# Column sums of V's weights by DMA and GpSimd, block 3 turned by DMA, and a new order of the first loads

## The chip, the core and the metric

The kernel runs on one core of one Trainium2 chip. A core has TensorE (matrix products, which accumulate in PSUM), VectorE, ScalarE and GpSimd (elementwise work) and SyncE, which only issues transfers (DMAs). ScalarE and GpSimd can issue transfers too. Each engine runs its own list of instructions in order and waits for the others through semaphores. The metric is device time of one execution in microseconds; lower is better. In the profile the engines are called PE, DVE, ACT, POOL and SP, and PEld is TensorE's loading of weights.

## The reference

From one input x (2048 rows of 512, bf16) two branches are computed on the normalized rows, and added to x:

```python
xn = _layernorm(x, axis=-1)
return x + _A_ref(xn, A_wqkv, A_wo) + _B_ref(xn, B_w_in, B_w_sp, B_b_sp, B_w_out)
```

Branch A is attention with 32 heads of 16 values, in which row s looks at the 8 rows s, s-2, ..., s-14: q, k and v are xn times wqkv, the logits are q·k/4, a softmax runs over the 8 rows (those before row 0 are masked), the weighted sum of v follows, and then the product with wo. Branch B takes z = gelu(xn w_in), split in z1 and z2 of 896 columns each; z2 is normalized along its row; g = w_sp z2 + b_sp mixes the 2048 rows; and (z1 * g) w_out is the branch's result.

## The kernel before

**Tiling.** The 2048 rows are 16 blocks of 128 (index b), and 4 groups j of four blocks. xn is needed turned (512 values on partitions, rows along the free side), as xnT. Everything lies in one on-chip array, `arena`, of which regions are used again for other things later; `fpool` holds small float32 values, and PSUM has 8 banks of 512 float32 values per partition.

**Stages on TensorE.** First 8 matmuls on constants (`warm`, L560). Then for each block V (L654, `v_block`) and z2 (L766, `z2_block`), for each group Q and K (L677, `qk_pair`), then z1 (L812), then g = w_sp z2 (L907, from 98 us on), then the output blocks (L963, L972). L713 (`logits`) sums, for two groups at a time, the products of q and k over the 16 values of a head.

**Layer norm.** `ln_block(b)` takes the statistics of a block on VectorE (L599 `bnst`, L601 `bnag`, L609 `vpe`), 1/sqrt on GpSimd (L611 `rstd`), and normalizes on VectorE (L623 `norm`). Blocks 0 to 3 (`NXT`) are then turned by TensorE against a unit matrix (L579, `xTr`) and copied to xnT by ScalarE (L587, `xTe`); blocks 4 to 15 are turned by a DMA that SyncE issues (L617, `xTd`).

**V of blocks 0 and 1.** These two don't wait for their norm. The raw rows are turned (L579, `xTx`), copied by ScalarE (L606, `xTc`) and multiplied with V's weights (`wv`). As (x - m) r W = r (x W - m s), with s the column sums of W, the sums are needed: `colsum` multiplies a matrix of ones with `wv` on TensorE (L638, `cs_0` and `cs_1`, 4 matmuls), which leaves s on every partition, and ScalarE copies -s (L642, `cse`). VectorE adds -s m in PSUM (L660, `fix`), and ScalarE multiplies by r on the way out (L663, `Ve`). GpSimd then issues the store of the block's V to DRAM (L668, `Vw`; scratch `vscr`), from where SyncE loads shifted rows back for the attention sum (L930).

**VectorE's long part.** For each j and each of 4 sets of heads, one product of 4096 values per partition (L698) and, from the second set on, one sum (L703); L713 of groups 0 and 1 needs all eight products and six sums. The second norm works in waves of four blocks (`z2_wave`): four tiny steps on VectorE (L785 to L792), 1/sqrt on GpSimd (L795, `zr`), four normalizations on VectorE (L798, `zn`).

**What sets the order.** `Plan.schedule` simulates all engines with estimated durations (`est`), a model of the transfers, and the landing times in `land` for the first loads; at each step it places the task that can start first, and among those within `tol` ns the one with the smallest `prio`. VectorE's next task may begin `overlap` ns before the estimated end of the last. The result is one fixed list for each engine. For the opening the order is written out by hand (L1003 to L1012); `after` and these lists add order without a wait. The waits that the engines really carry out follow from the data alone. A task that uses PSUM gets a bank when it is placed.

**First loads.** SyncE issues wv in two halves, x of block 2, the two halves of w_in's second part (`w_in2a`, `w_in2b`, for z2), x of blocks 3 to 7, Q's weights, K's weights and x of blocks 8 to 15; ScalarE issues x of blocks 0 and 1. After the turns of blocks 4 to 15 come the turned loads of w_sp (L880), with w_in's first part (L853) among them.

## Time and profile before

| | us |
|---|---|
| median of 3 runs (lowest, highest) | 237.30 (237.21, 237.56) |
| span of the profiled execution, from first to last instruction | 236.1 |
| around the span (the runs' times less the span) | 1.1 to 1.5 |
| PE busy | 231.7 (98%) |
| DVE busy | 207.4 (88%) |
| ACT busy | 96.5 (41%) |
| POOL busy | 32.7 (14%) |
| granted TensorE clock | 1.000 |

The profile is of one execution. It gives no total time of that execution, so its span stands beside the three runs. In the lines of a timeline below, the first number is the start in us from the beginning of the span, the second the time from the start of the first instruction of the line to the end of its last, then come engine, line of the program, operation, output<-input with its shape, and the count; in square brackets stands how long the engine was idle before it, and what ended that. In a line of waits stand who waited, for whom, the total in us, how often, and the longest. Matmuls overlap: one is shown with 0.38 us, while the next starts 0.215 us after it.

### The profile page before, as it was taken

The page shows a single profiled execution, that of the slowest core. Times are in us where ns is not written, and L with a number is a line of the kernel's source. Part 1 is how long each engine was busy: PE and PEld are TensorE (multiplying, and loading weights), DVE is VectorE, ACT ScalarE, POOL GpSimd, SP SyncE. Part 2 cuts the span into 40 slices and gives each one's busy share as a digit, 9 for nine tenths or more (in the row PEclk, how much of TensorE's full clock was granted, in tenths as well). Part 3 has the DMA queues.
Part 4 walks back from the last instruction along what each step waited for, and adds up shares of the span by engine and source line. Part 5 has one row for each costly group of instructions (what it writes and reads, how often), then busy time and mean ns, then how long its engine had stood idle before and what let it go on. Part 6 is the DMA issues. An engine that isn't in the chain of part 4 may idle for free.

```text
span 236.1 us, 2974 instructions
## 1 busy us (share of the span) xinstructions
PE 231.7 (98%) x1114; PEld 109.1 (46%) x1135; DVE 207.4 (88%) x269; ACT 96.5 (41%) x145; POOL 32.7 (14%) x56
## 2 busy tenths in 40 slices
PE   8999999999999999999999999999999999999996
PEld 3455555555444444444444444444444444444443
DVE  3799899999998899999699998986989997999432
ACT  3598889888967895510120531111111111000000
POOL 2259650311733100000000000000000000000000
PEclk9999999999999999999999999999999999999999
DMA  7998969991048325430999999998995959936432
GB/s 211 352 283 163 243 146 217 195 202 44 22 165 260 92 85 69 104 118 0 226 347 252 225 266 180 200 304 187 346 258 175 261 161 303 193 95 181 135 96 69
DMA packets 82013, 43.86 MB, mean 186 GB/s; under 512 B 54336, under 2 KB 81360, under 8 KB 82000
## 3 DMA queue, kind: packets, MB, share of 16 engines
q1 hardware_dynamic: 80768, 41.27, 71.5%
q0 software_dynamic: 800, 2.11, 2.8%
q10 hardware_dynamic: 432, 0.30, 0.6%
q8 instruction: 9, 0.15, 0.3%
q14 instruction: 4, 0.03, 0.1%
HBM read 26.35 MB, written 4.21 MB: 129 GB/s over the span
## 4 chain that ended last, share of the span: by engine, by line
PE 94%; DMA 3%; SPq 1%; ACT 1%; issue 1%; DVE 0%
PE ps L907 41%; PE ps L677 12%; PE ps L972 10%; PE ps L812 10%; PE ps L766 9%; PE ps L963 6%; PE ps L654 5%; DMA arena<-in_B_w_in_dram 3%; PE ps L713 1%; ACT arena L774 0%; SPq L518 0%; ACT arena L587 0%; PE ps L579 0%; SPq L514 0%; SPq L524 0%
## 5 line engine op out<-in xcount | busy, mean ns | idle before, releaser
L907 PE MATMUL ps<-arena 128*128 128x512 bf16 x439 | 96.6, 379 | 0.5
L907 PEld LDWEIGHTS ps<-arena 128*128 128x128 bf16 x448 | 43.7, 98 | 53.1 <-issue 0.4
L915 ACT ACTIVATE arena<-ps 128x1024 bf16<-128x1024 f32 (+1 forms) x16 | 14.7, 917 | 78.0 <-PE ps L907 78.0
L698 DVE TENSOR_TENSOR arena<-arena 128x4096 bf16<-128x4096 bf16 x16 | 36.5, 2282 | 0.1
L935 DVE TENSOR_TENSOR arena<-arena 128x4096 bf16<-128x4096 bf16 x16 | 36.4, 2283 | 0.0
L938 DVE TENSOR_TENSOR arena<-arena 128x2048 bf16<-128x2048 bf16 (+1 forms) x32 | 29.9, 948 | 0.0
L677 PE MATMUL ps<-arena 128*128 128x512 bf16 x126 | 28.7, 379 | 0.1
L703 DVE TENSOR_TENSOR arena<-arena 128x4096 bf16<-128x4096 bf16 x12 | 27.4, 2287 | 0.1
L972 PE MATMUL ps<-arena 128*128 128x512 bf16 (+2 forms) x117 | 26.9, 366 | 0.1
L766 PE MATMUL ps<-arena 128*128 128x448 bf16 x128 | 26.0, 352 | 0.5 <-DMA arena<-in_B_w_in_dram 0.5
L812 PE MATMUL ps<-arena 128*128 128x512 bf16 x110 | 24.4, 379 | 0.1
L978 DVE TENSOR_TENSOR arena<-ps,arena 128x512 bf16<-128x512 f32 (+2 forms) x17 | 11.2, 658 | 11.7 <-PE ps L972 11.7
L677 PEld LDWEIGHTS ps<-arena 128*128 128x128 bf16 x128 | 14.5, 113 | 13.0
L766 PEld LDWEIGHTS ps<-arena 128*128 128x128 bf16 x128 | 12.3, 98 | 12.7 <-ACT arena L642 0.7
L686 ACT ACTIVATE arena<-ps 128x1024 bf16<-128x1024 f32 x16 | 16.3, 1021 | 4.4 <-PE ps L677 4.1
L972 PEld LDWEIGHTS ps<-arena 128*128 128x128 bf16 x119 | 11.4, 98 | 12.8
L812 PEld LDWEIGHTS ps<-arena 128*128 128x128 bf16 x112 | 10.9, 98 | 13.2 <-ACT arena L818 0.3
L963 PE MATMUL ps<-arena 128*128 128x512 bf16 (+2 forms) x66 | 16.5, 366 | 0.1
L774 ACT ACTIVATE arena<-ps 128x896 bf16<-128x896 f32 x16 | 14.6, 914 | 3.2 <-PE ps L766 3.1
L818 ACT ACTIVATE arena<-ps 128x1024 bf16<-128x1024 f32 (+1 forms) x16 | 13.9, 923 | 4.9 <-PE ps L812 4.8
L654 PE MATMUL ps<-arena 128*128 128x512 bf16 x60 | 15.6, 379 | 0.2
L779 ACT ACTIVATE arena<-arena 128x896 bf16<-128x896 bf16 x16 | 15.1, 945 | 0.0
(61 smaller groups left out, 168.5 us busy)
## 6 DMA issues: line engine op xcount, KB each, us to landing
arena<-vscr SPq DMA_DIRECT2D x16, 1024.0 KB, 7.1
arena<-in_A_x_dram SPq DMA_DIRECT2D x30, 128.0 KB, 3.6
vscr<-arena POOLq DMA_DIRECT2D x16, 128.0 KB, 3.0
out_dram<-arena SPq DMA_DIRECT2D x15, 128.0 KB, 1.8
arena<-in_A_wqkv_dram SPq DMA_DIRECT2D x2, 512.0 KB, 6.9
arena<-in_B_w_in_dram SPq DMA_DIRECT2D x2, 448.0 KB, 6.1
arena<-in_B_w_in_dram SPq DMA_DIRECT2D x1, 896.0 KB, 5.9
arena<-in_B_w_out_dram SPq DMA_DIRECT2D x1, 896.0 KB, 4.9
```

Of the source, the lines that this page charges most:

```text
L654: last = t.matmul(P(bk, 512), A("xcT", 128, 512 * b + 128 * dc) if b < 2 else xTv(b, dc), A("wv", 512, 512 * dc), start=(dc == 0), stop=(d ...
L677: last = t.matmul(P(bk, 512, 512 * which), AC(off["wqk"] + 2048 * which + 512 * dc + c, [[4, 128]]), AC(off["xnT"] + dc * S + 512 * j, [[1 ...
L686: T("act", lambda a: a.activation(AC(qo, [[ko - qo, 2], [1, 512]]), P(bk, 1024).rearrange("p (t n) -> p t n", t=2), ACTF.Copy, scale=0.5), ...
L698: T("dve", (lambda pbv, qb, kb: lambda v: v.tensor_tensor(pbv, qb, kb, ALU.mult))(pbv, qb, kb), reads=rd, writes=[("pb", s_)], est=c_tt(40 ...
L703: T("dve", (lambda av, bv: lambda v: v.tensor_tensor(av, av, bv, ALU.add))(av, bv), reads=[("pb", 1)], writes=[("pb", acc)], est=c_tt(4096 ...
L766: last = t.matmul(P(bk, 448, 512 * hf), xTv(b, dc), AC(off["w_in2"] + 896 * dc + 448 * hf, [[1, 448]]), start=(dc == 0), stop=(dc == 3))
L812: last = t.matmul(P(bk, 512, 512 * i), AC(off["w_in1"] + 896 * dc + 128 * fc, [[1, 128]]), AC(off["xnT"] + dc * S + 512 * j, [[1, 512]]), ...
L907: last = t.matmul(P(bk, 512, 512 * i), AC(off["z2"] + FH * sh + 128 * fc, [[1, 128]]), AC(off["wT%d" % r_] + sh * 512, [[1, 512]]), start= ...
L935: T("dve", lambda v: v.tensor_tensor(tv, tv, av, ALU.mult), reads=[("attn", b)], writes=[("Vs", sv)], est=c_tt(4096), name="pv%d" % b, pri ...
L938: T("dve", (lambda n: lambda v: v.tensor_tensor(A("Vs", n, 4096 * sv), A("Vs", n, 4096 * sv), A("Vs", n, 4096 * sv + n), ALU.add))(n), wri ...
L963: last = t.matmul(P(bk, cn), AC(off["OT"] + 512 * tb + 128 * cc, [[1, 128]]), AC(off["wo"] + 512 * cc + c0, [[1, cn]]), start=(cc == 0), s ...
L972: last = t.matmul(P(bk, cn), AC(off["z1T"] + fc * S + 128 * tb, [[1, 128]]), AC(off["w_out"] + 512 * fc + c0, [[1, cn]]), start=False, sto ...
```

## The change

Column sums. The four matmuls and ScalarE's copy are gone. SyncE issues four DMA transposes of wv within the chip, after the turns of blocks 4 to 15, which lays the 512 columns on 128 partitions, 4 to each. GpSimd adds up along the free side in nine steps of halved width (256 to 1, four rows at once), writes the 512 sums to a DRAM scratch (`cscr`), and SyncE reads them back to every partition (`csb`).

V. Blocks 0 to 3 (`NRAW`) are now computed from raw rows. ScalarE multiplies by r on the way out of PSUM into a float32 copy (`vraw`), and VectorE adds the correction s(-m r), with -m r from one small operation (`mr`), and writes the bf16 block; this frees the PSUM bank without waiting for s. V of blocks 0 and 1 runs in four single matmuls with a wait each. wv comes in three loads (1, 1, 2 quarters).

Block 3. `NXT` is 3: block 3 is turned by DMA, and its transfer is issued after the load of block 5 and ahead of those of blocks 6 to 15.

Loads. x of block 0 in two halves on two queues; x of block 3 ahead of w_in's second part; Q's and K's weights as one transfer of 1 MB, issued by ScalarE between the copies of block 2 and block 3 (`xTc2_0`, `xTc3_0`). One of the two short warm-up matmuls is gone.

Planner. Transposes count 1270 or 2200 ns of issue and 900 ns of latency, `tol` is 20 for 50, `overlap` 10 for 40, and `land` has new values.

```diff
@@ -216,12 +216,12 @@
...
-                t.eng_end = r + iss
+                t.eng_end = r + (t.dma.get("iss") or iss)
...
-                t.end = xe + dma_lat
+                t.end = xe + (900.0 if t.dma.get("xbar") else dma_lat)
@@ -348,12 +348,14 @@
...
-    NXT = 4
-    NWARM = 8
+    NXT = 3
+    NRAW = 4
+    NWARM = 7
...
+    cscr = nc.dram_tensor("cscr", (512,), F32).ap()
@@ -490,7 +505,7 @@
         def dma(eng, fn, nbytes, chan, reads=(), writes=(), name="", xbar=False, prio=0.0, after=()):
...
-                     dma=dict(chan=chan, nbytes=nbytes, xbar=xbar))
+                     dma=dict(chan=chan, nbytes=nbytes, xbar=xbar, iss=(1270.0 if nbytes < 400000 else 2200.0) if xbar else None))
@@ -532,27 +546,27 @@
...
-        def ld_wqk(which, eng):
-            dma(eng, lambda e: e.dma_start(
-                AC(off["wqk"] + 2048 * which, [[512, 4], [1, 512]]),
-                A_wqkv[:, 512 * which: 512 * which + 512].rearrange("(c p) n -> p c n", p=128)),
-                512 * 512 * 2, ("wqk", which), writes=[("wqk", which)], name="ld%s" % ("qk"[which]))
-
-        dma("act", lambda e: e.dma_start(A("xin", 512), x2[0:128, :]), 128 * 512 * 2, ("xin", 0),
-            writes=[("xin0", 0), ("xin0", 1)], name="ldx0")
+        def ld_wqk(eng):
+            dma(eng, lambda e: e.dma_start(A("wqk", 4096).rearrange("p (c n) -> p c n", c=4),
+                                           A_wqkv[:, 0:1024].rearrange("(c p) n -> p c n", p=128)),
+                512 * 1024 * 2, "wqk", writes=["wqk"], name="ldqk")
+
+        for h, q_ in enumerate(("sp", "act")):
+            dma(q_, (lambda h: lambda e: e.dma_start(ar[64 * h:64 * h + 64, off["xin"]:off["xin"] + 512],
+                                                     x2[64 * h:64 * h + 64, :]))(h),
+                64 * 512 * 2, ("xin0", h), writes=[("xin0", h)], name="ldx0%s" % "ab"[h])
...
-        ld_wv(0)
-        ld_wv(1)
+        for d0, dn in ((0, 1), (1, 1), (2, 2)):
+            ld_wv(d0, dn)
...
+        ld_x(3, "sp")
...
-        ld_x(3, "sp")
...
-        ld_wqk(0, "sp")
-        ld_wqk(1, "sp")
+        ld_wqk("act")
@@ -600,12 +614,13 @@
...
-            if b < 2:
+            if b < NRAW:
...
-                for hf in range(2):
-                    T("act", (lambda hf: lambda a: a.activation(A("xcT", 256, 512 * b + 256 * hf), P(bc, 256, 256 * hf),
-                                                                ACTF.Copy))(hf),
-                      reads=[bc], writes=[("xcT", b, hf)], est=c_act(256), name="xTc%d_%d" % (b, hf), prio=-1)
+                for h0, hn in ((0, 1), (1, 1)) if b < 2 else ((0, 2),):
+                    T("act", (lambda h0, hn: lambda a: a.activation(A("xcT", 256 * hn, 512 * b + 256 * h0),
+                                                                    P(bc, 256 * hn, 256 * h0), ACTF.Copy))(h0, hn),
+                      reads=[bc], writes=[("xcT", b, hf) for hf in range(h0, h0 + hn)], est=c_act(256 * hn),
+                      name="xTc%d_%d" % (b, h0), prio=-1)
@@ -629,42 +644,68 @@
         def xTv(b, dc):
...
+        def FT(o_, n):
+            return A("cst", 2048).bitcast(F32).rearrange("p (c k) -> p c k", c=4)[:, :, o_:o_ + n]
+
         def colsum():
-            bk = plan.bank("cs")
-            for hf in range(2):
-                def mm(t, hf=hf):
-                    last = None
-                    for dc in (2 * hf, 2 * hf + 1):
-                        last = t.matmul(P(bk, 512), ones[:, 0:128], A("wv", 512, 512 * dc), start=(dc == 0),
-                                        stop=(dc == 3))
-                    return last
-                T("pe", mm, reads=[("wv", hf)], writes=[bk], est=2 * c_mm(512) * (1 if hf else 2), name="cs_%d" % hf, prio=2)
-            T("act", lambda a: a.activation(ncs, P(bk, 512), ACTF.Copy, scale=-1.0), reads=[bk],
-              writes=["ncs"], est=c_act(512), name="cse", prio=-0.5)
+            for dc in range(4):
+                dma("sp", (lambda dc: lambda e: e.dma_start_transpose(AC(off["wvT"] + 128 * dc, [[512, 4], [1, 128]]),
+                                                                      A("wv", 512, 512 * dc)))(dc),
+                    128 * 512 * 2, ("wvT", dc), reads=[("wv", dc)], writes=[("wvT", dc)], name="wvT%d" % dc, xbar=True,
+                    prio=2, after=lnd[4:])
+            n, prev = 256, "wvT"
+            while n:
+                if n == 256:
+                    a_, b_ = (AC(off["wvT"] + o_, [[512, 4], [1, n]]) for o_ in (0, n))
+                else:
+                    a_, b_ = (FT(o_, n) for o_ in (0, n))
+                T("pool", (lambda n, a_, b_: lambda g: g.tensor_tensor(FT(0, n) if n > 1 else Fv("cs", 4).rearrange(
+                    "p (c k) -> p c k", k=1), a_, b_, ALU.add))(n, a_, b_),
+                  reads=[("wvT", dc) for dc in range(4)] if n == 256 else ["cst"] if n == 1 else [],
+                  writes=["cst"] if n > 1 else ["cs"], est=200 + 4.2 * n, name="csum%d" % n, prio=1, after=lnr)
+                n //= 2
+            dma("pool", lambda e: e.dma_start(bass.AP(tensor=cscr.tensor, offset=cscr.offset, ap=[[1, 128], [128, 4]]),
+                                              Fv("cs", 4), allow_slow_non_contiguous=True),
+                2048, "cswr", reads=["cs"], writes=["cscr"], name="csw", prio=1)
+            dma("sp", lambda e: e.dma_start(csb, bass.AP(tensor=cscr.tensor, offset=cscr.offset, ap=[[0, 128], [1, 512]])),
+                128 * 2048, "csrd", reads=["cscr"], writes=["csb"], name="csr", prio=2)
+
+        def vraw(b):
+            return A("vraw", 1024, 1024 * b).bitcast(F32)
+
+        def hd(x):
+            return x.rearrange("p (h d) -> p d h", d=16)
+
+        def mean_rstd():
+            T("dve", lambda v: v.scalar_tensor_tensor(
+                Fv("mr", NRAW), Fv("mv", 2 * NRAW).rearrange("p (b t) -> p b t", t=2)[:, :, 0], -1.0, Fv("rstd", NRAW),
+                ALU.mult, ALU.mult),
+              reads=[("mv", b) for b in range(NRAW)] + [("rstd", b) for b in range(NRAW)], writes=["mr"], est=160,
+              name="mr", prio=1)
         def v_block(b):
...
-            for hf in range(2):
-                def mm(t, hf=hf):
+            for dcs in ((0,), (1,), (2,), (3,)) if b < 2 else ((0, 1), (2, 3)):
+                def mm(t, dcs=dcs):
...
-                    for dc in (2 * hf, 2 * hf + 1):
-                        last = t.matmul(P(bk, 512), A("xcT", 128, 512 * b + 128 * dc) if b < 2 else xTv(b, dc),
+                    for dc in dcs:
+                        last = t.matmul(P(bk, 512), A("xcT", 128, 512 * b + 128 * dc) if b < NRAW else xTv(b, dc),
...
-                T("pe", mm, reads=[("xcT", b, hf) if b < 2 else ("xnT", b), ("wv", hf)], writes=[bk],
-                  est=2 * c_mm(512) * (1.5 if (b, hf) == (0, 0) else 1), name="V%d_%d" % (b, hf), prio=(2 if b < 4 else 60 + b))
-            if b < 2:
-                T("dve", lambda v: v.scalar_tensor_tensor(P(bk, 512), ncs, Fv("mv", 1, 2 * b), P(bk, 512),
-                                                          ALU.mult, ALU.add),
-                  reads=["ncs", ("mv", b)], writes=[bk], est=690, name="fix%d" % b, prio=1)
-            T("act", lambda a: a.activation(vn.rearrange("p (d h) -> p d h", d=16),
-                                            PC(bk.col(), [[1, 16], [16, 32]]), ACTF.Copy,
-                                            scale=Fv("rstd", 1, b) if b < 2 else 1.0),
-              reads=[bk] + ([("rstd", b)] if b < 2 else []), writes=[("Vn", sl)], est=c_act(512), name="Ve%d" % b,
-              prio=4)
+                T("pe", mm, reads=[("xcT", b, dcs[0] // 2) if b < NRAW else ("xnT", b)] + [("wv", dc) for dc in dcs],
+                  writes=[bk], est=len(dcs) * c_mm(512), name="V%d_%d" % (b, dcs[0]), prio=(2 if b < 4 else 60 + b))
+            vdh = vn.rearrange("p (d h) -> p d h", d=16)
+            if b < NRAW:
+                T("act", lambda a: a.activation(vraw(b), P(bk, 512), ACTF.Copy, scale=Fv("rstd", 1, b)),
+                  reads=[bk, ("rstd", b)], writes=[("vraw", b)], est=c_act(512), name="Ve%d" % b, prio=4)
+                T("dve", lambda v: v.scalar_tensor_tensor(vdh, hd(csb), Fv("mr", 1, b), hd(vraw(b)), ALU.mult, ALU.add),
+                  reads=["csb", "mr", ("vraw", b)], writes=[("Vn", sl)], est=690, name="fix%d" % b, prio=6)
+            else:
+                T("act", lambda a: a.activation(vdh, PC(bk.col(), [[1, 16], [16, 32]]), ACTF.Copy),
+                  reads=[bk], writes=[("Vn", sl)], est=c_act(512), name="Ve%d" % b, prio=4)
@@ -675,11 +716,11 @@
...
-                                        AC(off["wqk"] + 2048 * which + 512 * dc + c, [[4, 128]]),
+                                        AC(off["wqk"] + 1024 * dc + 512 * which + c, [[4, 128]]),
...
-                T("pe", mm, reads=[("wqk", which)] + [("xnT", b) for b in range(4 * j, 4 * j + 4)], writes=[bk],
+                T("pe", mm, reads=["wqk"] + [("xnT", b) for b in range(4 * j, 4 * j + 4)], writes=[bk],
@@ -823,11 +864,12 @@
...
-        lnd = [ln_block(b) for b in range(2)]
+        lnd = [ln_block(b) for b in range(NRAW)]
+        lnd += [ln_block(b) for b in range(NRAW, NB)]
+        mean_rstd()
...
-        v_block(0)
-        v_block(1)
-        lnd += [ln_block(b) for b in range(2, NB)]
+        for b in range(NRAW):
+            v_block(b)
@@ -1001,22 +1043,21 @@
...
-                      ["xTx0", "cs_0", "V0_0", "xTx1", "cs_1", "V0_1", "xTr0", "V1_0", "xTr1", "V1_1",
-                       "z2_0_0", "z2_0_0b", "z2_0_1", "xTr2", "z2_1_0", "z2_1_1", "V2_0", "V2_1", "xTr3", "z2_2_0"],
-                      ("rstd4", "Vw0"),
-                      ("bnst0", "bnag0", "vpe0", "bnst1", "bnag1", "vpe1", "norm0", "norm1", "bnst2", "bnag2",
-                       "vpe2", "norm2", "fix0", "bnst3", "bnag3", "vpe3", "fix1", "norm3", "bnst4", "bnag4", "vpe4",
-                       "bnst5"),
+                      ["xTx0", "xTx1", "V0_0", "V0_1", "V1_0", "V1_1", "V0_2", "xTx2", "V0_3", "V1_2", "V1_3", "xTx3", "V2_0", "V2_2",
+                       "xTr0", "V3_0", "V3_2", "xTr1", "z2_0_0", "z2_0_0b", "z2_0_1", "xTr2", "z2_1_0", "z2_1_1", "z2_2_0"],
+                      ("bnst0", "bnag0", "vpe0", "bnst1", "bnag1", "vpe1", "norm0", "bnst2", "bnag2", "vpe2", "norm1", "bnst3",
+                       "bnag3", "vpe3", "norm2", "norm3", "bnst4", "bnag4", "vpe4", "mr", "bnst5"),
...
-                      ("xTc0_0", "xTc0_1", "xTc1_0", "xTc1_1", "xTe0_0", "xTe0_2", "cse", "xTe1_0", "xTe2_0", "z2g0",
-                       "Ve0", "xTe3_0", "z2g1", "Ve1", "Ve2", "z2s0"), ("V10_1", "Q3_3")):
+                      ("xTc0_0", "xTc0_1", "xTc1_0", "xTc1_1", "xTc2_0", "ldqk", "xTc3_0", "xTe0_0", "xTe0_2", "Ve0", "xTe1_0", "Ve1", "xTe2_0", "Ve2",
+                       "z2g0", "Ve3", "z2g1", "z2s0"), ("ldx5", "xTd3", "ldx6"),
+                      *[("xTd3", "ldx%d" % b) for b in range(7, NB)], ("V10_2", "Q3_3")):
...
-        plan.schedule(tol=50.0, dma_bw=300.0, dma_lat=1600.0, overlap=40.0,
-                      land=dict(ldx0=3580.0, ldx1=4700.0, ldwv0=4050.0, ldwv1=5300.0, ldx2=5700.0, ldwin2a=6950.0, ldwin2b=8250.0,
-                                ldx3=8650.0, ldx4=9050.0, ldx5=9400.0, ldx6=9750.0, ldx7=10200.0, ldq=11700.0, ldk=13200.0))
+        plan.schedule(tol=20.0, dma_bw=300.0, dma_lat=1600.0, overlap=10.0,
+                      land=dict(ldx0a=3350.0, ldx0b=3400.0, ldwv0=4050.0, ldx1=4050.0, ldwv1=4400.0, ldwv2=5060.0, ldx2=5400.0, ldx3=5750.0, ldwin2a=7700.0,
+                                ldwin2b=9300.0, ldx4=10400.0, ldx5=11100.0, xTd3=12300.0, ldqk=13100.0))
```

48 lines of the change are left out of this document (30 added, 18 removed).

## The prediction

> **What bounds the kernel now.** I read the chain that ended last first, then TensorE's waits, then the timelines of the first 12 us and of 26 to 66 us. The chain by engine, and all that TensorE waited for:
>
> ```profile
> PE 94%; DMA 3%; SPq 1%; ACT 1%; issue 1%; DVE 0%
> ...
> PE ps L560 <- PEq L1055: 0.8, 1, 0.8
> PE ps L766 <- DMA arena<-in_B_w_in_dram: 0.5, 2, 0.3
> ```
>
> TensorE sets the end and hardly ever waits. So the time is its first real instruction, plus its work, plus what it loses, and the losses lie in the opening:
>
> ```profile
> 3.73 0.61 PE L579 MATMUL ps<-arena 128*128 128x128 bf16 x4
> 4.26 0.85 PE L638 MATMUL ps<-arena,const-bfloat16-1.0 128*128 128x512 bf16 x2
> 4.95 0.60 PE L654 MATMUL ps<-arena 128*128 128x512 bf16 x2
> ...
> 7.34 0.59 PE L654 MATMUL ps<-arena 128*128 128x512 bf16 x2
> 8.22 0.92 PE L766 MATMUL ps<-arena 128*128 128x448 bf16 x4 [0.28 <-DMA arena<-in_B_w_in_dram]
> 9.34 0.93 PE L766 MATMUL ps<-arena 128*128 128x448 bf16 x4 [0.21 <-DMA arena<-in_B_w_in_dram]
> 10.11 0.39 PE L579 MATMUL ps<-arena 128*128 128x128 bf16 x4
> ```
>
> Starts tell the pitch: 5.38 to 5.60 is 0.22 for four 128-column turns, 5.60 to 6.03 is 0.215 per 512-column matmul, and the chain's 32 of L766 in 6.05 us are 0.189 per 448 columns. From 3.73 until xTr2 at 10.27 in the chain, the work is 4 turns, 12 wide matmuls and 8 of 448: 0.88 + 2.58 + 1.51 = 4.97 us in 6.54 us. So 1.57 us are lost there, and none later that counts.
>
> The second place that matters is where TensorE needs VectorE: L713, the head sums, takes the last product sum (L703).
>
> ```profile
> 60.90 2.29 DVE L703 TENSOR_TENSOR arena<-arena 128x4096 bf16<-128x4096 bf16 x1
> ...
> 64.64 1.05 PE L713 MATMUL ps<-arena 128*32 128x512 bf16 x16
> ```
>
> VectorE is done at 63.19 and L713 starts at 64.64: a margin of 1.45 us. VectorE is busy 25.9 of the 26 us before. TensorE works in order, so what VectorE is late beyond its margin there is added to the end.
>
> The third is what a small GpSimd operation costs beside those products:
>
> ```profile
> 26.73 2.53 POOL L611 TENSOR_TENSOR fpool<-fpool 128x1 f32<-128x1 f32 x1 [0.86 <-DVE fpool L609]
> 32.20 3.05 POOL L795 TENSOR_TENSOR fpool<-fpool 128x4 f32<-128x4 f32 x1 [2.94 <-DVE fpool L792]
> 45.34 3.05 POOL L795 TENSOR_TENSOR fpool<-fpool 128x4 f32<-128x4 f32 x1 [10.09 <-DVE fpool L792]
> ...
> 76.62 1.04 POOL L795 TENSOR_TENSOR fpool<-fpool 128x4 f32<-128x4 f32 x1
> ```
>
> The same L795 takes 1.04 us beside VectorE's PSUM work and 3.05 us beside a 4096-wide product: it ends 0.9 us after the product (45.23 + 2.29 = 47.52; 48.39). The product holds it back.
>
> **The change, part by part: the opening.** TensorE loses 4 matmuls with ones (4 x 0.215 = 0.86) and xTr3 (0.22), and gains xTx2 and xTx3 (0.44): -0.64 us. Block 0 comes in two halves on two queues and one 128-column warm-up matmul goes (0.1 us): the first turn waited for its load until 3.73; between 0 and 0.4 us earlier, I take 0.2. V2 and V3 move ahead of L766, 4 x 0.43 = 1.73 us of work to cover the arrival of w_in's second half (8.2 and 9.3). The new list has 1.32 (xTx0 to 3, xTr0, xTr1) plus 3.44 (V0 to V3) before it; begun at 3.5 it needs it at 8.3 at the earliest. Of the 1.57 us lost, the slow first microsecond stays (cs_0's two matmuls start at 4.26 and V0 at 4.95, 0.69 for 0.43), as does the wait for block 1 and its copy (0.33 per half, L606): about 0.8. New is that ScalarE issues Q's and K's load between two copies. Issuing the two took SyncE 0.44 and 0.99 us, so one takes 0.4 to 1.4; I take 0.7. xTc3 and V3 are that much later, of which TensorE's work on V2 and xTr0 covers some 0.3. Losses after: about 1.25, a gain of 0.3. Opening: -0.64 - 0.2 - 0.3 = **-1.15 us** (-0.5 to -1.7).
>
> Block 3's turn by DMA can start when norm3 is done, some 9.4 us (four blocks at the 1.02 us from 3.71 to 4.73, three norms of 0.41, the last rstd of 0.56). Landing takes 2.4 to 5.9 us by L617's rows: 11.8 to 15.3. TensorE wants it after z2_2, at about 14. Nearest is the median of 4.3, 13.7: hidden; the far end costs 1.3. The 1 MB of Q and K lands by 13.5 if the 350 GB/s of 7 to 14 us hold. SyncE is taken for 1.27 us by this turn, and the ten loads of blocks 6 to 15 are issued behind it from 10.7 instead of from 5.3 (blocks 6, 7) and 7.83 (8 to 15). At 0.54 us each (4.31 for 8) they end at 16.1, where before the turns began at 14.49. VectorE read block 6 at 13.5; it now lands at about 13.5 to 14, so the two correction steps of 0.75 us taken from VectorE here save nothing. ScalarE loses cse and xTe3 and gains xTc2, xTc3 (0.6 each): even.
>
> **The change: the column sums.** Turns of blocks 4 to 15 (16.2 us for twelve before, and w_in1's 0.5) end at 32.8; then four turns of V's weights, 1.35 each, to 38.2. They push w_sp's loads (L880, from 31.33) 7 us back; those are first read at 98 and before had all been issued by 50.9, so this is free. The last turn lands about 40.5 (39.3 to 42.8). Now nine adds run on GpSimd, over 4 x 511 = 2044 pairs. By GpSimd's memsets (0.195 for 128, 0.1 for 4: 0.75 ns each) they would take 2.4 us, by the one selecting row (L505, 0.292 for 128: 1.5 ns) 4.0; a two-input add is nearer the second. I take 4.0: 3.3 for the first four, 0.7 for the rest. Each that meets a product waits until it ends, about one step per product. Four products lie between 40.5 and the normalization at 49.76 (from 40.57, 42.90, 45.23 and 47.55).
>
> Whether an add holds up the product behind it, no row shows: 0 to 3.3 us on VectorE. Queued behind the nine adds on GpSimd are the issue of the write (0.57) and the L795 that was ready at 45.34; VectorE's L798 at 49.76 needs that one. So VectorE stops there for the rest of the adds with their handovers (1.2), the issue (0.57) and L795 (1.04), 2.8 us. VectorE is late by 2.8 to 6.1 us.
>
> The sums then go out as 512 single values and come back. The write takes 1.9 to 4.0 us by the stores of V (rows of 1 KB); I take 4, for many small pieces. The read takes 1.6 (a small store) to 4.9 (b_sp's 512 KB broadcast); I take 3. They are there at about 59 to 63. Four corrections of 0.75 (L660's row; 3.0 us, 1.5 more than before, and 0.16 for mr) wait for them on VectorE, ahead of the last products and of L713. SyncE waits at the read for the write; behind it are only w_sp's loads.
>
> What absorbs it: the margin of 1.45, and that the planner now counts 30 ns more per VectorE operation (overlap 40 to 10), some 79 of them from block 6 to L713, so that it puts L713 2.4 us later than VectorE needs and fills TensorE with other work. Together 3.8. The planner knows the corrections' own 3.0 us, but not the hold-ups. TensorE waits 0 (late by 2.8) to 2.3 (6.1) by L795, and 0 to 3.6 by the sums (63 + 3.0 + two to three products of 2.3 against a place at about 69). Both go by the held-up VectorE; I take **+2.5 us**.
>
> The Trainium skill, SBUF — State Buffer, section "SBUF: two separate sides", says that VectorE and GpSimd share a port pair as an exclusive lock, against a GpSimd operation that reads SBUF also for VectorE operations with two SBUF inputs, and that whichever starts first holds it for its whole instruction. The trace agrees for GpSimd waiting (3.05 against 1.04 us); that VectorE waits too no row here shows, and by this rule the upper end of 6.1 holds, without it the rival of no wait. Its GPSIMD Engine Reference, section 3.1, gives 4497 ns for an add of 2048 pairs; by it the adds take about 5.4 us in place of 4.0, and the wait would be 1.4 longer.
>
> **The sum.** The profiled execution spans 236.1 us; the three times are 237.21 to 237.56, so 1.1 to 1.5 us lie around the span, and I count against the median, 237.3. 237.3 - 1.15 + 2.5 = **238.6**.
>
> **The rivals.**
> - The chain of adds is covered. If adds do not hold up products, VectorE is late by 2.8, below the 3.8, and only the opening shows: 237.3 - 1.15 = 236.1 (235.5 to 236.8). It decides at a lateness of 3.8 us. For it: L698 behind the L795 of 45.34 took its usual 2.29.
> - The opening gains nothing, by block 3: its turn goes beside Q's and K's megabyte, lands at 15.3 and costs 1.3 at L677, with the adds covered: 237.4. Against it: before, the first of L677 came at 15.31 behind a similar queue without a wait.
> - The sums come far later: the adds at the longer end, 5.0 for the write of 512 pieces and 4.9 for the read, and ScalarE's copy of V8, which now has to wait for block 0's corrected V to leave its buffer, behind it. 5 to 6 us at L713: 241.5.
>
> **How the numbers follow.** Covered 0.34; same 0.11; a wait of 1 to 4 us at L713 0.42; the far one 0.13. The point is the third, 238.6 (own range 237.8 to 240.2). Leaving a tenth out on each side gives 235.6 to 241.8. Within 0.2% (0.5 us) is about what a measurement of this kernel can tell from no change. Faster takes the covered case and a little of the third, less the tail of it that falls within 0.5 us: 0.35; same 0.11; slower 0.54.
>
> **What would show it.** In the changed profile, the chain should contain a piece of VectorE or GpSimd at L713's new place, about 66 to 72 us, with TensorE's wait of 1 to 4 us there; GpSimd's adds should take 2 to 4 us each while products run, and products beside them more than 2.29; VectorE should sit idle ahead of a normalization (L798's new line) for GpSimd, and perhaps ahead of the first correction for a DMA. z2's first matmul should start at 9 to 10 us with V0 to V3 behind it. No wait at the head sums makes it wrong by the first rival; a wait at the first Q by block 3 or Q's and K's load, by the second; a wait at any other place would be one that I have not seen.

## The result, and the profile after

| | before | after |
|---|---|---|
| median (lowest to highest), us | 237.32 (237.06 to 237.56), 6 runs | 249.01 (245.78 to 251.8), 6 runs |
| span of the profiled execution, us | 236.1 | 248.6 |
| PE busy, us | 231.7 (98%) | 232.7 (94%) |
| GpSimd (POOL) busy, us | 32.7 | 45.5 |
| mean granted TensorE clock | 1.000 | 0.986 |

The changed kernel is slower: ratio 1.0392, interval 1.0356 to 1.0427. Ratios here count only runs within 1.5% of each kernel's fastest, so this one is below the ratio of the medians, and one run of those below, of 354.99 us at a granted clock of 0.663, stays out of its ratio. The execution profiled here took 249.85 us, about 4 us more than the fastest of the changed kernel.

TensorE still does the same work but no longer fills the chain that ended last. Its parts by engine, from the page of the changed kernel:

```profile
PE 73%; DMA 12%; POOL 6%; SPq 3%; issue 2%; DVE 2%; ACT 1%; POOLq 0%; DVEq 0%; ACTq 0%
```

What TensorE waited for in the changed kernel (who waited, for whom, total in us, times, longest):

```profile
PE ps L695 <- ACT arena L707: 10.8, 2, 7.9
PE ps L593 <- DMA arena<-in_A_x_dram: 1.1, 2, 0.8
```

Before, no wait but the first was over 0.3 us. Now V's matmuls (L695, before L654) wait 10.8 us, in stops of 2.90 and 7.87, for ScalarE's copies of V out of PSUM (L707, before L663). In the first stop no sum is involved: the copy at its end stands on ScalarE behind a copy of Q and K (L727), and that one waited 2.21 us for a product on VectorE (L739), which was late by then, as shown further down. The timelines of VectorE and of ScalarE:

```profile
62.51 2.29 DVE L739 TENSOR_TENSOR arena<-arena 128x4096 bf16<-128x4096 bf16 x1
```

```profile
64.83 1.02 ACT L727 ACTIVATE arena<-ps 128x1024 bf16<-128x1024 f32 x1 [2.21 <-DVE arena L739]
65.75 0.59 ACT L707 ACTIVATE arena<-ps 128x512 bf16<-128x512 f32 x1
```

For the second stop, the chain shows what the copy waited for, in order of time (start, us, what):

```profile
42.40 4.16 POOL arena L662
...
46.63 3.28 POOL arena L662
...
49.98 2.67 POOL arena L662
...
54.78 0.92 POOL fpool L836
55.70 11.45 DMA cscr<-fpool
...
67.17 4.19 DMA arena<-cscr
...
71.39 2.13 DVE arena L704 x2
...
73.80 7.04 DMA vscr<-arena
...
81.36 0.60 ACT arena L707
...
82.00 1.89 PE ps L695 x4
```

Read it downwards: the nine additions (L662) run from 42.40 to 54.78, the write of the sums takes 11.45, the read 4.19, two corrections (L704) follow, then block 1's corrected V is stored, which takes 7.04. Only then may ScalarE copy block 9's V, which uses the same buffer, and with this copy and the one behind it TensorE gets PSUM banks. VectorE itself was late for the corrections: its product before them ended at 69.45, and it waited only 1.94 us more for the sums:

```profile
71.39 2.12 DVE L704 SCALAR_TENSOR_TENSOR arena<-arena,fpool 128x512 bf16<-128x512 f32 x2 [1.94 <-DMA arena<-cscr]
```

TensorE's timeline of the changed kernel has the two stops and what comes after them:

```profile
66.40 1.90 PE L695 MATMUL ps<-arena 128*128 128x512 bf16 x8 [2.90 <-ACT arena L707]
...
82.00 1.89 PE L695 MATMUL ps<-arena 128*128 128x512 bf16 x4 [7.87 <-ACT arena L707]
83.82 1.90 PE L754 MATMUL ps<-arena 128*32 128x512 bf16 x16
```

After the long stop the four V matmuls take 1.82 us (82.00 to 83.82) where four took 0.86, and the head sums (L754, before L713) 1.90 where they took 0.98. The windows view of the changed kernel gives the reason (behind PE, PEld, DVE, ACT and POOL busy come the granted clock, the DMA share and GB/s):

```profile
76.00:78.00 2.00, 0.00 (x0) 0.00 (x0) 2.00 (x3) 0.60 (x1) 1.51 (x3) 1.00 0.83 278
78.00:80.00 2.00, 0.00 (x0) 0.00 (x0) 1.97 (x2) 0.00 (x0) 0.09 (x1) 0.69 0.96 355
80.00:82.00 2.00, 0.00 (x0) 0.00 (x1) 1.71 (x1) 1.14 (x3) 0.24 (x1) 0.50 0.19 73
82.00:84.00 2.00, 2.00 (x8) 0.57 (x12) 0.17 (x1) 1.83 (x5) 1.73 (x4) 0.50 0.38 148
84.00:86.00 2.00, 1.84 (x17) 0.52 (x11) 0.23 (x2) 1.07 (x2) 1.76 (x4) 0.60 0.47 186
86.00:88.00 2.00, 2.00 (x10) 0.87 (x9) 2.00 (x4) 1.22 (x2) 0.33 (x1) 1.00 0.37 146
```

The clock was 1.00 until 78 us, in the stop, and then 0.50 until about 85.5. So the accounts of this execution close: 10.8 of waits, 1.9 at the lowered clock (0.96 and 0.92), and -0.14 in the opening (the first Q at 15.17, before 15.31) make 12.5, the difference of the two spans (248.6 less 236.1).

The opening, TensorE's timeline of the changed kernel from its first turn to the first Q:

```profile
3.46 0.49 PE L593 MATMUL ps<-arena 128*128 128x128 bf16 x4
4.75 0.40 PE L593 MATMUL ps<-arena 128*128 128x128 bf16 x4 [0.80 <-DMA arena<-in_A_x_dram]
4.99 1.46 PE L695 MATMUL ps<-arena 128*128 128x512 bf16 x5
6.73 0.40 PE L593 MATMUL ps<-arena 128*128 128x128 bf16 x4 [0.28 <-DMA arena<-in_A_x_dram]
...
10.01 1.86 PE L807 MATMUL ps<-arena 128*128 128x448 bf16 x8
...
15.17 1.03 PE L718 MATMUL ps<-arena 128*128 128x512 bf16 x4
```

It starts 0.27 us earlier, has 0.64 us less work, and arrives 0.14 us earlier: 0.77 us of new loss, first of all the wait for block 1, whose turn now stands with nothing between it and block 0's.

VectorE and GpSimd between 42 and 58 us in the changed kernel; the two timelines:

```profile
42.28 2.29 DVE L744 TENSOR_TENSOR arena<-arena 128x4096 bf16<-128x4096 bf16 x1
44.49 2.09 DVE L833 TENSOR_TENSOR fpool<-fpool 128x4 f32<-128x4 f32 x1
46.50 2.28 DVE L739 TENSOR_TENSOR arena<-arena 128x4096 bf16<-128x4096 bf16 x1
48.81 3.24 DVE L744 TENSOR_TENSOR arena<-arena 128x4096 bf16<-128x4096 bf16 x1
55.79 1.05 DVE L839 TENSOR_SCALAR arena<-arena,fpool 128x896 bf16<-128x896 bf16 x2 [3.73 <-POOL fpool L836]
```

```profile
54.73 1.02 POOL L836 TENSOR_TENSOR fpool<-fpool 128x4 f32<-128x4 f32 x1
55.70 0.94 POOL L667 DMA_DIRECT2D cscr<-fpool  x1
```

They hold each other up, in both directions. The first addition starts at 42.40, 0.12 us after a product sum, and ends at 46.56; the sum ends at 44.57, so 2.0 us of its 4.16 are its own. Then VectorE's tiny L833, which takes 0.15 elsewhere, takes 2.09 and ends as the addition ends; and the sum at 48.81 takes 3.24 in place of 2.29, beside the second addition. In the same way the other two large ones have 1.13 and 0.60 of their own; with the six small ones (0.47 to 0.20) that is 5.45 us of adding spread over 12.4. VectorE then stops 3.73 us for L836, which stands behind the additions: it normalizes at 55.79, before at 49.76.

### The profile page after: what moved, and what is told of

Same layout as the page of the kernel before. It is cut to its first block, busy times and chain, and to the rows that moved or that the text cites. A ratio compares the mean times of both kernels' runs of the same rounds, so it can differ in the third digit from the quotient of the medians.

```text
span 248.6 us, 2995 instructions
## 1 busy us (share of the span) xinstructions
PE 232.7 (94%) x1114; PEld 108.8 (44%) x1134; DVE 213.0 (86%) x272; ACT 96.5 (39%) x145; POOL 45.5 (18%) x66
## 4 chain that ended last, share of the span: by engine, by line
PE 73%; DMA 12%; POOL 6%; SPq 3%; issue 2%; DVE 2%; ACT 1%; POOLq 0%; DVEq 0%; ACTq 0%
PE ps L949 39%; PE ps L853 10%; PE ps L1014 10%; PE ps L1005 6%; POOL arena L662 5%; DMA cscr<-fpool 5%; DMA vscr<-arena 3%; PE ps L718 3%; PE ps L807 3%; PE ps L695 2%; DMA arena<-arena 2%; DMA arena<-cscr 2%; SPq L652 2%; DMA arena<-in_A_x_dram 1%; POOL fpool L626 1%
## 5 line engine op out<-in xcount | busy, mean ns | idle before, releaser
L739 DVE TENSOR_TENSOR arena<-arena 128x4096 bf16<-128x4096 bf16 x16 | 36.4, 2278 | 0.1
L744 DVE TENSOR_TENSOR arena<-arena 128x4096 bf16<-128x4096 bf16 x12 | 28.4, 2364 | 0.1
L695 PE MATMUL ps<-arena 128*128 128x512 bf16 x61 | 16.5, 396 | 11.1 <-ACT arena L707 10.8
L727 ACT ACTIVATE arena<-ps 128x1024 bf16<-128x1024 f32 x16 | 16.3, 1019 | 8.1 <-DVE arena L739 4.8
L807 PEld LDWEIGHTS ps<-arena 128*128 128x128 bf16 x128 | 12.3, 98 | 11.9 <-DMA arena<-in_B_w_in_dram 0.4
L1014 PEld LDWEIGHTS ps<-arena 128*128 128x128 bf16 x119 | 11.4, 98 | 12.8
L960 DVE TENSOR_TENSOR arena<-arena 128x1024 bf16<-128x1024 bf16 (+1 forms) x16 | 9.9, 621 | 8.1 <-ACT arena L957 8.0
```

Source lines behind the costliest of these rows:

```text
L695: last = t.matmul(P(bk, 512), A("xcT", 128, 512 * b + 128 * dc) if b < NRAW else xTv(b, dc), A("wv", 512, 512 * dc), start=(dc == 0), stop ...
L727: T("act", lambda a: a.activation(AC(qo, [[ko - qo, 2], [1, 512]]), P(bk, 1024).rearrange("p (t n) -> p t n", t=2), ACTF.Copy, scale=0.5), ...
L739: T("dve", (lambda pbv, qb, kb: lambda v: v.tensor_tensor(pbv, qb, kb, ALU.mult))(pbv, qb, kb), reads=rd, writes=[("pb", s_)], est=c_tt(40 ...
L744: T("dve", (lambda av, bv: lambda v: v.tensor_tensor(av, av, bv, ALU.add))(av, bv), reads=[("pb", 1)], writes=[("pb", acc)], est=c_tt(4096 ...
L807: last = t.matmul(P(bk, 448, 512 * hf), xTv(b, dc), AC(off["w_in2"] + 896 * dc + 448 * hf, [[1, 448]]), start=(dc == 0), stop=(dc == 3))
L1014: last = t.matmul(P(bk, cn), AC(off["z1T"] + fc * S + 128 * tb, [[1, 128]]), AC(off["w_out"] + 512 * fc + c0, [[1, cn]]), start=False, sto ...
```

## The experiments

Theory A at the outset: the opening is worth little, and all of the loss hangs on the chain from the additions to block 1's store. Rival: something else in the change (raw V of blocks 0 to 3, the planner's new numbers, the opening) costs by itself.

**Sums on TensorE.** All of the change, but four matmuls with ones and a copy by ScalarE make the sums, behind z2 of block 2.

```diff
-            for dc in range(4):
-                dma("sp", (lambda dc: lambda e: e.dma_start_transpose(AC(off["wvT"] + 128 * dc, [[512, 4], [1, 128]]),
...
-                T("pool", (lambda n, a_, b_: lambda g: g.tensor_tensor(FT(0, n) if n > 1 else Fv("cs", 4).rearrange(
...
+            bk = plan.bank("cs")
+            for hf in range(2):
...
+                        last = t.matmul(P(bk, 512), ones[:, 0:128], A("wv", 512, 512 * dc), start=(dc == 0),
...
+            T("act", lambda a: a.activation(csb, P(bk, 512), ACTF.Copy), reads=[bk], writes=["csb"], est=c_act(512),
...
-                       "xTr0", "V3_0", "V3_2", "xTr1", "z2_0_0", "z2_0_0b", "z2_0_1", "xTr2", "z2_1_0", "z2_1_1", "z2_2_0"],
+                       "xTr0", "V3_0", "V3_2", "xTr1", "z2_0_0", "z2_0_0b", "z2_0_1", "xTr2", "z2_1_0", "z2_1_1", "z2_2_0", "cs_0", "cs_1"],
```

> Changed kernel with the column sums back on TensorE (four matmuls with ones behind the first half of block 2's z2, copied by ScalarE); the raw V of blocks 0 to 3, the new loads and block 3's turn by DMA stay. Theory A (all that was lost came from the sums arriving at 71 us): TensorE's waits of 2.90 and 7.87 us go, and what is left is the new opening, 0.14 us ahead at the first Q in the profile, plus 4 x 0.215 us of matmuls: 237.3 - 0.14 + 0.86 = 238.0 (237.4 to 238.5). Theory B (another part does it: block 3's turn, the corrections after PSUM, the planner's new numbers): 241 or more.

238.77 us (238.28 to 239.64), ratio 1.0078 (1.0052 to 1.0104). A holds, a little above its range. The sums, with the engines that they hold up, are the loss; what is left is 0.8% slower than before, though TensorE's only waits in its opening are these (behind the first 0.8 us of any kernel here):

```profile
PE ps L686 <- DMA arena<-in_A_wqkv_dram: 0.5, 2, 0.3
PE ps L798 <- DMA arena<-in_B_w_in_dram: 0.2, 1, 0.2
```

Its first Q starts at 15.53 with 20 of block 0 to 2's 24 z2 matmuls done (before: 15.31 with 24), so 4 x 0.189 = 0.76 us of work is behind it: on equal work 0.98 later, of which 0.22 is one turn more. The spans differ by as much, 237.1 against 236.1. So the new opening, with the ones in it, is about 1 us worse than the old.

**Own buffers.** The corrected V of blocks 0 to 3 goes to four buffers of its own, so that blocks 8 and 9 need not wait for their stores.

```diff
+            R1(("Vr", s_), "attn", 512, 512 * s_)
...
-            vn = A("Vn" if sl < 4 else "bbc", 512, 512 * (sl % 4))
+            vn = A("attn" if b < NRAW else "Vn" if sl < 4 else "bbc", 512, 512 * (sl % 4))
```

> Changed kernel, but the corrected V of blocks 0 to 3 gets buffers of its own, so that ScalarE's copies of V8 and V9 no longer wait for the stores of V0 and V1. Theory A (the sums are late for everything behind them): the 7.87 us wait goes, but TensorE then waits at L754 for the last product sum, which ended at 79.4 where TensorE had got to 74.1: 5 us there, the 2.9 us before it stay; 241 to 244. Theory C (the buffer alone turns a late sum into a wait): 237 to 239.

247.21 us (246.13 to 248.25), ratio 1.043 (1.0394 to 1.0466): above both expectations, and no gain that can be told from the changed kernel. The wait at V is gone, and another stands in its place, at the head sums:

```profile
PE ps L757 <- DVE arena L747: 7.0, 1, 7.0
```

That is the wait that the prediction had in mind, at the place that it named, with 7.0 us where it had 1 to 4. The buffer was only where the delay was met first. Nor is it the late sums alone: VectorE, held up here too (it normalizes at 55.15), waits only 2.34 us for them.

**Pieces of 16 bytes.** The sums are laid out so that each partition writes its four values as one piece: 128 pieces in place of 512; the correction reads them in the new order.

```diff
-            dma("pool", lambda e: e.dma_start(bass.AP(tensor=cscr.tensor, offset=cscr.offset, ap=[[1, 128], [128, 4]]),
-                                              Fv("cs", 4), allow_slow_non_contiguous=True),
+            dma("pool", lambda e: e.dma_start(bass.AP(tensor=cscr.tensor, offset=cscr.offset, ap=[[4, 128], [1, 4]]),
+                                              Fv("cs", 4)),
```

> Changed kernel, but the sums are written as 128 pieces of 16 bytes instead of 512 of 4, and read in that order by the correction. Theory A1 (the number of pieces makes the write slow, 11.4 us from issue to landing): it lands in 3 to 4 us, the sums come 7 us earlier, and the two waits of TensorE shrink by 3 to 6 us together: 239.5 to 242.5. Theory A2 (GpSimd's queue is held up whatever it writes): landing stays above 9 us and the time at 245 to 249.

245.01 us (243.91 to 246.68), ratio 1.0322 (1.0277 to 1.0367). The write lands in 2.4 us in place of 11.4, as theory A1 has it, and the sums are there about 9 us sooner; the time falls by 4.0 us in the medians, and by 0.7% in the ratios (whose intervals overlap), less than A1 expected. The corrections start at 69.12, 2.3 us earlier than before the edit: VectorE, late as it is, has them behind its products in its list. So the write by itself is worth some 4 of the 11.7 us between the medians, and the first stop, in which no sum is involved, stays, with 2.60. TensorE's waits (behind its clock of 0.50 for some 3 us after two of them) are smaller and in three places:

```profile
PE ps L695 <- ACT arena L709: 2.8, 2, 2.6
PE ps L855 <- ACT arena L709: 2.1, 1, 2.1
PE ps L756 <- DVE arena L746: 0.9, 1, 0.9
```

**One reduction on VectorE** in place of the nine additions.

```diff
-            n, prev = 256, "wvT"
-            while n:
...
+            T("dve", lambda v: v.tensor_reduce(Fv("cs", 4), AC(off["wvT"], [[512, 4], [1, 512]]), AX.X, ALU.add),
+              reads=[("wvT", dc) for dc in range(4)], writes=["cs"], est=2300, name="csum", prio=1)
```

> Changed kernel, but one reduction on VectorE (2048 values, about 2.3 us) takes the place of the nine adds on GpSimd, 12.4 us from first to last. The write stays as it is. If the adds' share is what the profile shows, GpSimd is free for the second norm's 1/sqrt, VectorE does not stop for it (3.73 us), the sums come 8 to 10 us earlier (61 to 63 us), and the time is 238 to 240.5. If the write and the read alone decide, it stays above 243.

242.72 us (242.32 to 243.85), ratio 1.0249 (1.0219 to 1.0278): between the two expectations. The reduction takes 2.29 us, no addition is there to hold VectorE up, and the write is issued at 45.89 in place of 55.70. But its 512 pieces take 11.2 us again, to 57.1; the read, behind a turn of w_sp on SyncE, is issued at 57.68 and takes 6.2, and VectorE meets the same chain further down (waits of VectorE):

```profile
DVE arena L695 <- DMA arena<-cscr: 4.9, 1, 4.9
```

**The write from SyncE's queue**, with 512 pieces as in the change.

```diff
-            dma("pool", lambda e: e.dma_start(bass.AP(tensor=cscr.tensor, offset=cscr.offset, ap=[[1, 128], [128, 4]]),
+            dma("sp", lambda e: e.dma_start(bass.AP(tensor=cscr.tensor, offset=cscr.offset, ap=[[1, 128], [128, 4]]),
```

> The change with the write of the 512 sums issued by SyncE in place of GpSimd, still as 512 pieces of 4 bytes; the read stands right behind it on SyncE. Theory A: the number of pieces is what takes 11.4 us, whatever queue: landing in 8 to 12 us, 247 to 251 in all. Theory B: it is GpSimd's queue that is slow with small pieces: landing in 2 to 4 us, and the time of the variant with 128 pieces, 244 to 246.5.

251.57 us in one run; the landing, from the view of the write's line:

```profile
DMA to landing us min/median/max: 12.1/12.1/12.1
```

Theory A, with both numbers a little above its ranges: the pieces take the time, whichever queue issues them.

**The short chain.** VectorE's reduction, 128 pieces, the read on GpSimd's queue right behind the write, and own buffers, together; the diff shows the one edit not shown yet.

```diff
-            dma("sp", lambda e: e.dma_start(csb, bass.AP(tensor=cscr.tensor, offset=cscr.offset, ap=[[0, 128], [1, 512]])),
+            dma("pool", lambda e: e.dma_start(csb, bass.AP(tensor=cscr.tensor, offset=cscr.offset, ap=[[0, 128], [1, 512]])),
```

> The change with its whole sum chain shortened at once: one VectorE reduction (2.29 us) in place of nine GpSimd additions, the sums written as 128 pieces of 16 bytes, read back from GpSimd's own queue (behind the write, not behind SyncE's turns of w_sp), and the corrected V of blocks 0 to 3 in buffers of their own. Theory A: the chain of the sums and the buffer that V8 and V9 wait for are all of the loss; what is left is the opening, which the variant with the sums on TensorE showed at 238.77; less the four matmuls with ones (4 x 0.215 = 0.86) this is 237.9 (237.3 to 238.6), with no TensorE wait above 0.5 us after the opening. Theory B: VectorE's added work (2.29 for the reduction, 4 x 1.06 for the corrections) is by itself more than the slack at the head sums: 239.5 to 242.5, with TensorE waiting for VectorE's last product sum.

237.84 us (237.56 to 239.2), ratio 1.005 (1.0029 to 1.007). Theory A, at its number. With the chain short, the change is 11 us faster than as made, and 0.9 us slower than before. Where that is, its waits of TensorE and two pieces of its chain show:

```profile
PE ps L594 <- DMA arena<-in_A_x_dram: 0.5, 1, 0.5
PE ps L714 <- DMA arena<-arena: 0.4, 1, 0.4
PE ps L1001 <- DMA arena<-arena: 0.3, 1, 0.3
PE ps L689 <- DMA arena<-in_A_wqkv_dram: 0.3, 1, 0.3
```

```profile
205.69 2.42 DMA arena<-arena
208.11 1.01 PE ps L1001 x4
```

Its first Q starts at 15.20, 0.11 us ahead of before. Then group 1's first Q (L714) waits 0.4 us for a turn of blocks 4 to 7, and the output (L1001) for the last turns of the attention sum: there, near the end, the chain leaves TensorE, which in the kernel before it does not.

The rest of the runs ask where the opening's gain went.

**Old first loads in the short chain**: x of block 0 whole, wv in two halves, TensorE's first list and the planner's landing times put to match.

```diff
-        for h, q_ in enumerate(("sp", "act")):
...
+        dma("act", lambda e: e.dma_start(A("xin", 512), x2[0:128, :]), 128 * 512 * 2, ("xin", 0),
...
-        for d0, dn in ((0, 1), (1, 1), (2, 2)):
+        for d0, dn in ((0, 2), (2, 2)):
...
-                      ["xTx0", "xTx1", "V0_0", "V0_1", "V1_0", "V1_1", "V0_2", "xTx2", "V0_3", "V1_2", "V1_3", "xTx3", "V2_0", "V2_2",
+                      ["xTx0", "V0_0", "V0_1", "xTx1", "V0_2", "V0_3", "V1_0", "V1_1", "V1_2", "V1_3", "xTx2", "xTx3", "V2_0", "V2_2",
```

> The same short chain with the first loads as before the change: x of block 0 whole from ScalarE's queue and wv in two halves, and TensorE's first list put to match (block 0's first V matmuls between the turns of blocks 0 and 1). Theory A: the change's opening gained nothing because two more transfers at the head of the queues made block 1 and V's weights land later; then this is 0.4 to 0.9 us faster than the short chain with the new loads, near 237.2, and V1 ends earlier. Theory B: the loads do not matter, the four matmuls with ones had filled a wait that is there in any case: within 0.3 us of it.

239.44 us (238.05 to 240.45), ratio 1.0107 (1.0078 to 1.0135): 1.6 slower than the short chain, against both theories. It isn't the opening: from 76.05 us on TensorE is in the same z1 matmuls as the short chain from 75.99. Its chain too leaves TensorE near 205 us, over VectorE and a transfer of 3.38 us. The runs spread over 2.4 us, and why VectorE's end differs so much between them was not found.

**The new first loads alone, in the kernel before**: x of block 0 in halves on two queues, wv in three loads, and their landing times for the planner.

```diff
-        dma("act", lambda e: e.dma_start(A("xin", 512), x2[0:128, :]), 128 * 512 * 2, ("xin", 0),
...
+        for h, q_ in enumerate(("sp", "act")):
...
-        ld_wv(0)
-        ld_wv(1)
+        for d0, dn in ((0, 1), (1, 1), (2, 2)):
+            ld_wv(d0, dn)
```

> The kernel before with one part of the change alone: x of block 0 in two halves on two queues, and wv in three loads (1, 1, 2 quarters); nothing else. Theory A: V's weights land about 0.5 to 1 us later and TensorE waits for them: 0.2 to 1.0 us slower than before. Theory B: the earlier start of block 0 counts (0.27 us in the traces): 0 to 0.3 us faster.

238.95 us in the median of six (238.70 without the run of 354.99), ratio 1.009 (1.0069 to 1.0112): about 2 us slower, twice the upper end of theory A. Block 0 starts at 3.56 rather than 3.73, but the ones need half of wv, which comes 1 us later (waits of TensorE):

```profile
PE ps L639 <- DMA arena<-in_A_wqkv_dram: 1.1, 1, 1.1
```

The late load isn't all of it. Behind that wait, from 5.25 to 8.84, TensorE takes 3.59 us for 8 wide matmuls and 4 turns, which are 1.94 us of work: the wide ones start about 0.42 us apart in place of 0.215, though the granted clock of the windows view reads 1.00. So 1.65 us are lost to the slow pace here; in the kernel before, the slow first microsecond cost 0.26.

**The ones at their old place**, in the variant with the sums on TensorE.

```diff
-                      ["xTx0", "xTx1", "V0_0", "V0_1", "V1_0", "V1_1", "V0_2", "xTx2", "V0_3", "V1_2", "V1_3", "xTx3", "V2_0", "V2_2",
-                       "xTr0", "V3_0", "V3_2", "xTr1", "z2_0_0", "z2_0_0b", "z2_0_1", "xTr2", "z2_1_0", "z2_1_1", "z2_2_0", "cs_0", "cs_1"],
+                      ["xTx0", "V0_0", "V0_1", "cs_0", "xTx1", "V1_0", "V1_1", "cs_1", "V0_2", "xTx2", "V0_3", "V1_2", "V1_3", "xTx3", "V2_0", "V2_2",
+                       "xTr0", "V3_0", "V3_2", "xTr1", "z2_0_0", "z2_0_0b", "z2_0_1", "xTr2", "z2_1_0", "z2_1_1", "z2_2_0"],
```

> The change with the sums on TensorE as in the first variant (238.77), but the four matmuls with ones at their old place, between the turns of blocks 0 and 1 and the first matmuls of V, in place of behind the second norm's block 2. Theory A: before, these matmuls cost TensorE nothing, since they filled its wait for block 1 and for V's weights: 0.5 to 0.9 us below that variant, about 238.0. Theory B: they cost their 0.86 us wherever they stand: 238.5 to 239.

239.49 us (238.37 to 242.38), ratio 1.0105 (1.0077 to 1.0133): nothing gained; theory B's number or a little worse. Under the new loads V's weights come so late that the ones wait as well (0.38 us for wv ahead of the second pair).

**Without the ones, in the kernel before** (the sums are left out).

```diff
-            bk = plan.bank("cs")
-            for hf in range(2):
...
+            T("pool", lambda g: g.memset(ncs, 0.0), writes=["ncs"], est=450, name="cse", prio=-3)
```

> The kernel before without the four matmuls with ones and without ScalarE's copy of the sums; GpSimd sets the buffer of the sums to zero early, so the corrections of V of blocks 0 and 1 take place on VectorE as before, but subtract nothing (the column sums are left out). It prices the largest term of my opening by itself. Theory A: the four matmuls filled TensorE's wait for block 1, for V's weights and for w_in, and cost next to nothing: 236.7 to 237.1, with longer waits named ahead of z2. Theory B, my prediction's term: they cost 4 x 0.215 = 0.86: 236.0 to 236.3.

237.8 us (237.11 to 238.45), ratio 1.0039 (1.0024 to 1.0054): slower than before by 0.9, and above both expectations. z2 begins at 8.07 where it began at 8.22, so 0.86 us of work less brought 0.15; and z2 of block 1 waits 0.69 us for a copy by ScalarE (L587), from which I took it that the planner had dealt it another bank. So the next run kept the banks.

**One of the four ones, in the kernel before.**

```diff
-            for hf in range(2):
+            for hf in range(1):
                 def mm(t, hf=hf):
...
-                        last = t.matmul(P(bk, 512), ones[:, 0:128], A("wv", 512, 512 * dc), start=(dc == 0),
...
+                    return t.matmul(P(bk, 512), ones[:, 0:128], A("wv", 512), start=True, stop=True)
```

> The kernel before with one of the four matmuls with ones in place of all four (three quarters of the column sums are left out); PSUM banks, ScalarE's copy and all else stay, since leaving all four out had also handed the second norm's block 1 a bank that ScalarE frees late. TensorE has 3 x 0.215 = 0.65 us less to do. Theory A: in the opening it only waits longer for loads and copies: 236.6 to 237.1, the first Q within 0.2 us of 15.31. Theory B, my prediction's term: 236.1 to 236.4, the first Q near 14.7.

237.11 us (236.5 to 237.87), 12 runs, against 237.17 before: ratio 0.9996 (0.9983 to 1.0009). Theory A in the time: 0.65 us of TensorE's work is worth nothing here. Waits in the profiled execution:

```profile
PE ps L762 <- DMA arena<-in_B_w_in_dram: 0.9, 2, 0.7
```

Before, the wait for w_in was 0.5. The first Q starts at 15.87, later than theory A's 15.5 at most: w_in landed later in this execution, the slowest of the twelve.

**Block 3 by DMA, and Q's and K's weights in one transfer, in the kernel before.**

```diff
-    NXT = 4
+    NXT = 3
...
-        ld_wqk(0, "sp")
-        ld_wqk(1, "sp")
+        ld_wqk("act")
...
+                      ("ldx5", "xTd3", "ldx6"),
```

> The kernel before with two parts of the change alone: block 3 turned by DMA, issued ahead of the loads of blocks 6 to 15, and Q's and K's weights in one transfer that ScalarE issues behind block 1's copies. Sums, V and the first loads as before. Theory A: these parts cost nothing and save block 3's turn on TensorE (0.22): 236.6 to 237.1. Theory B: the loads of blocks 6 to 15, issued some 5 us later, make the turns of later blocks late (the short chain showed TensorE waiting 0.36 us for block 4 to 7's turns at group 1's first Q): 237.4 to 238.4 with a wait at Q of group 0 or 1.

238.6 us (238.18 to 239.69), ratio 1.0075 (1.0055 to 1.0094). Theory B, a little above its range, with the wait where it says (group 1's first Q, L674), and one more at V of block 3 (L651), which is not raw here:

```profile
PE ps L651 <- DMA arena<-arena: 1.2, 1, 1.2
PE ps L674 <- DMA arena<-arena: 1.1, 1, 1.1
```

No version came out faster than the kernel before.

## Why the prediction was wrong

It said slower, which was right, and 238.6 within 235.6 to 241.8; it is 249.0. What failed is the price of the chain of the sums at TensorE: +2.5 us, where the profile has 10.8 of waits and 1.9 at a lowered clock. By its steps:

- **The write of the sums: 4 us taken, 11.45 measured.** This term was off by most. The prediction priced the write by the stores of V, whose rows are 1 KB, and put its longest value for "many small pieces". No row of before had a transfer of 4-byte pieces, and its upper bound, 5.0 in the rival, came from no row like it. With 128 pieces the same 2 KB took 2.4 us, from another queue 512 pieces took 12.1. But it isn't all of the error: with the write at 2.4, below the 4 taken, the changed kernel still took 245.01.
- **The additions: 4.0 taken, 5.45 measured, 12.4 from first to last.** The nearer row (L505) was too cheap for two inputs. By the Trainium skill, GPSIMD Engine Reference, section 3.1, which has 4497 ns for an add of 2048 pairs, the estimate was about 5.4, and the trace agrees.
- **The hold-ups: 2.8 to 6.1 us late, 6.0 measured** (55.79 against 49.76). Right, at its upper end. That end stood under the rule of the Trainium skill (SBUF — State Buffer, "SBUF: two separate sides") that VectorE waits for GpSimd too; L833's 2.09 us and L744's 3.24 show that it does.
- **The read: 3 taken, 4.2 measured; corrections: 0.75 each taken, 1.05 measured.** Both small beside the write. The sums were there at 71.4 in place of 59 to 63.
- **Where the wait falls.** The forecast put it at the head sums, 2.5 us, and counted 3.8 us of margin there. TensorE stopped before it got there, at V's matmuls, and twice. The first stop, 2.90, came from the held-up VectorE through ScalarE's copy of Q and K, a path that no step had; it stays (2.60) with 16-byte pieces. The second, 7.87, came through ScalarE's copies of V8 and V9 and the stores of blocks 0 and 1: the mechanism of the last rival, held for 0.13 and priced at 5 to 6 us. With own buffers, the wait stood at the head sums with 7.0. Two delays met in both places: VectorE, held up, came to the corrections at 69.45, and the sums at 71.4. So curing one leaves the other: 245.01 with the write short, 242.72 with the additions off GpSimd. A store of 7.04 us, where stores had been taken at 1.9 to 4.0, added to the second stop.
- **The lowered clock.** 1.9 us behind the stop; no step had it. By the windows above the clock was halved 4 to 5 us into a stop of 7.87. The six times of the changed kernel go with its mean granted clock: 245.8 and 245.9 us at 0.993, 248.2 to 251.8 at 0.986 to 0.979. The Trainium skill, TensorE: Matmul & The Clock Gate, section "Why this matters for your kernels", says that an idle gap of more than about 3 us ends at half rate; for this stop the trace agrees, and a forecast of a long wait should have had it in its price.
- **The opening: -1.15 taken, -0.14 measured.** The start (-0.2) was right: 3.46 against 3.73. The work (-0.64) was counted as if TensorE were busy there; but it waits for loads and copies, and three of the four matmuls with ones taken out alone were worth nothing (0.9996). The losses (-0.3) went the other way, +0.77. Two more transfers at the head of the queues made what lies behind them later, and TensorE was slow behind that wait (about 2 us together in the kernel before); block 3's transfer with the loads behind it costs up to 1.1 us at group 1's first Q (kernel before; 0.4 in the short chain, and no such wait is named in the changed kernel's profile). The prediction looked for that last one at group 0's Q, by its second rival, and priced the later loads by block 6's statistics alone. How much each of these holds in the changed kernel isn't settled, as these waits change from run to run.

The rival in which the chain is covered (236.1) fell by its own condition: VectorE was 6.0 us late, above the 3.8 at which it was to decide, and even the short chain ends at 237.84. The rival of block 3's turn fell too: the first Q came at 15.17, with no wait of TensorE named there. One reading was loose, and nothing hung on it: by 50.9 only eight of the sixteen loads of w_sp (L880) had been issued in the kernel before.

## What to carry to other kernels

Price a transfer by its number of pieces before its bytes (here 128 rows of 1 KB, V's stores in the kernel before, landed in 1.9 to 4.0 us, 128 pieces of 16 bytes in 2.4 and 3.3, and 512 of 4 bytes in 11.2 to 12.1; fewer pieces of 4 bytes were not run), and follow its data to the buffer that it must leave: a late value is paid at the first place where a shared buffer or bank makes an engine wait, and curing that place shows the next. Work taken from the bounding engine is worth something only in a stage where that engine doesn't wait for loads; in the opening the matmuls with ones were filling. And a small exact experiment (the same work on the old engine, the chain made short) separates a poor idea from a poorly built one: here the idea, with its chain made short, was still 0.5% slower.
